# Later scatters and earlier routing in a fused RWKV attention and expert kernel

## The chip, the cores and the metric

One NeuronCore of a Trainium2 chip runs the whole kernel. The metric is device microseconds of one execution; the figure for a kernel is the median of its runs. Before the change that is 402.42 us (three runs, 400.07 to 404.3).

## The reference

Two stages. The first is RWKV attention over batch 4, 8 heads, 768 steps, head size 48; the second sends each of the 3072 resulting rows through the one of 8 experts with the highest gate logit (rows of 384, hidden width 1024, float32).

```python
def _attn_ref(r, k, v, w, u):
    ...
    for t in range(S):
        ...
        cur = np.einsum('bhd,bhe->bhde', u[None] * kt, vt)
        y[:, :, t] = np.einsum('bhd,bhde->bhe', rt, state + cur)
        state = wt[:, :, :, None] * state + np.einsum('bhd,bhe->bhde', kt, vt)

def _moe_ref(x, w_gate, w1, w2):
    logits = x @ w_gate
    expert_idx = np.argmax(logits, axis=1)
    ...
    for e in range(E):
        xe = x[expert_idx == e]
        out[expert_idx == e] = gate_w[..., None] * (np.maximum(xe @ w1[e], 0.0) @ w2[e])
```

## The kernel before

**Attention.** The 768 steps are cut into 12 chunks of 64. A block is one chunk of two of the four batches, so there are 24 blocks (`NB`) of 128 rows, and even and odd blocks carry separate states `U`. For a block n, VectorE (DVE) forms running products of the decays forwards (`pre`, L351) and backwards (`suf`, L360) and scales the keys, `kh` (L368). GpSimd (POOL) forms `rh` (r times `pre`, L395) and `rk` (r times k, L387). TensorE (PE) multiplies the old state by `rh` (`pe_inter`, L481), forms the block's score matrix from `kh` and `rh` (`pe_a`, tile `ap`, L466, 32 products), the bonus coefficients from `rk` (`pe_kt`, L512 and L522, whose copy by ScalarE (ACT) is `ct`, L413) and the transposed keys (L518). DVE copies the masked scores into the tile `at` (L373), which already holds the diagonals of coefficients that ACT (L432) and POOL (L423, `pool_diag`) wrote there. PE multiplies `at` by the values (`pe_av`, L491, tile `yp`) and adds the block to the state (`pe_dp`, tile `U`, L501). ACT copies `yp` out as the block's rows, `xr` (L452), and PE transposes them in the next iteration (L529, `xT`).

**Routing.** Four blocks make a group (`GRP`), six groups in all (`NG`). While the next group's blocks run, the finished group G is routed: gate logits on PE (`logit_mm`, L536, copied out as `ls`), their transposition (`logit_tr`, L543, tile `lt`), the maximum and the one-hot row on DVE (`gate`, L560 to L564), the rank within the expert on PE (`rank`, L575 to L578), the row number on DVE (`place`, L587 and L590, tile `pi`), and then four scatters (L604). A scatter is an indirect DMA that POOL issues: 128 rows of 386 floats of `xr` go to the places `pi` of the buffer `xs`, which is sorted by expert. A tiny memset on POOL (L609) follows each. Before any scatter, `xs` is filled with zero rows by eight stores on SyncE's (SP) queue, issued in iterations 0 to 5 (`prefill`, L335).

**Order.** PE, DVE, ACT and POOL execute in the order in which the program is written; SP too. `iteration(n)` writes, for n from -2 to 22, the work of block n on PE together with the preparation of blocks n+1 and n+2 on the other engines; i is n modulo 4. On POOL that is `rh` of n+1, a scatter if one is due, `rk` of n+2 and the diagonal of n+1. `rk` waits for `kh` of n+1 by a dependence marked "one port" in the code. Block 23 and the last routing follow by hand ("the hand-over"), among the first row tile of expert work: its load `xg` from `xs` (L260), its transposed copies (L300 to L302) and its first products (`mm1`, L311). Weights of an expert are split into a high and a low part on ACT and DVE in pieces (`side`, L237 and L239). From about 157 us on only expert work runs.

Of the kernel before, what the change touches and what calls it, by code (L numbers as in the profile page):

```python
# [12 lines left out]
AF = mybir.ActivationFunctionType  # L13
ALU = mybir.AluOpType
# [6 lines left out]
C = 64  # L21
NS = S // C
NB = NS * 2
# [9 lines left out]
GRP = 4  # L33
# [9 lines left out]
FIRST = 3  # L43
# [12 lines left out]
def rwkv_moe_kernel(ctx, tc, rkw, vv, ub, wg, wr, w1, w2, out):  # L56
    nc = tc.nc
# [306 lines left out]
    def dve_kh(n):  # L364
        if real(n):
            d = blk[n]
            d["kh"] = work([RP, NSEG, C], F32, "kh")
            ch["kh"] = nc.vector.tensor_tensor(out=d["kh"], in0=d["k"], in1=d["suf"][:, :, 3:SEG], op=ALU.mult)  # L368
# [19 lines left out]
            if n > 1:  # L388
                after(i, ch["kh"], "one port")

    def pool_rh(n):
        if real(n):
            d = blk[n]
            d["rh"] = work([RP, NSEG, C], F32, "rh")
            nc.gpsimd.tensor_tensor(out=d["rh"], in0=d["r"], in1=d["pre"][:, :, 1:C + 1], op=ALU.mult)  # L395

    def act_pad(n):
        if real(n) and (n // 2) % SUP:
# [11 lines left out]
    def act_ct(n):  # L410
        if real(n):
            blk[n]["ct"] = ct = sm.tile([P, H], F32, name="ct", tag="ct", bufs=3)
            nc.scalar.activation(ct, blk[n]["cp"], AF.Copy)  # L413

    def act_cT(n):
        if real(n):
# [37 lines left out]
    def act_xT(n):  # L454
        if real(n):
            blk[n]["xT"] = t = xtp.tile([P, DM], F32, name="xT", tag="xT")
            nc.scalar.activation(t, blk[n]["xp"], AF.Copy)

    def pe_a(n):
        if real(n):  # L460
# [63 lines left out]
    def pe_xT(n, t):  # L524
        if real(n):
            G, i = divmod(n, GRP)
            blk[n]["xp"] = xp = t[:, 0:DM]
            for j in range(3):
                nc.tensor.transpose(xp[:, j * P:(j + 1) * P], ch["xr", G][:, i, j * P:(j + 1) * P], ident)  # L529
# [68 lines left out]
    def pool_ids(G):  # L598
        nc.gpsimd.tensor_copy(ch["xr", G].bitcast(I32)[:, :, DM + 1], tokid[:, 2 * G:2 * G + 2, :].rearrange("p s b -> p (s b)"))

    def scatter(G, bs):
        xr = ch["xr", G]
        for b in bs:
            i = nc.gpsimd.indirect_dma_start(out=xsf, out_offset=bass.IndirectOffsetOnAxis(ap=ch["pi", G, b], axis=0),  # L604
                                             in_=xr[:, b, :], in_offset=None, bounds_check=E * NTOK - 1, oob_is_err=False)
            for k in scat:
                tc.declare_no_dep(i.ins, k, reason="rows of different tokens")
            scat.append(i.ins)
            nc.gpsimd.memset(none, 0.0)  # L609
# [80 lines left out]
    for n in range(1, LD):  # L690
# [3 lines left out]
        if n == 2:  # L694
            nc.sync.dma_start(wgt, wg)

    def iteration(n):
        G, i = divmod(n, GRP)
        g = G - 1 if n >= 0 else -1
        whole = (g, 0, GRP)  # L700
        if 0 <= n < 6:
            for e in range(E * n // 6, E * (n + 1) // 6):
                prefill(e)
        if n >= 0:
            load(n + 6)
        full = 0 <= g < NG - 1
        if real(n):
            blk[n]["ap"] = psA.tile([P, 4, 256], F32, name="ap", tag="ap")
            pe_xT(n - 1, blk[n]["ap"][:, 1:3, :].rearrange("p a c -> p (a c)"))
            pe_inter(n)  # L710
            pe_a(n)
        dve_scale(n + 1)
        if full and i == 2:
            gate(whole)
        if full and i == 3:
            place(whole)
        act_pend(n + 1)
        act_g(n + 1)
        pool_rh(n + 1)
        dve_suf(n + 1)  # L720
        if n == -2:
            pool_rk(0)
        pe_kt(n)
        act_pad(n + 2)
        dve_kh(n + 1)
        dve_at(n)
        act_kt(n)
        act_ct(n + 1)
        if full and i == 3:
            scatter(g, (0,))  # L730
        if g > 0 and i < 3:
            scatter(g - 1, ((1,), (2,), (3,))[i] if g - 1 != FIRST else ((1,), (2, 3), ())[i])
        if n > -2:
            pool_rk(n + 2)
        pe_av(n)
        if n < 2:
            act_diag(n + 1, range(0, H if n < 0 else NQ))
        act_xr(n)
        act_xT(n - 1)
        if n == NB - 2:  # L740
            dve_diag(n + 1)
        elif n >= 2:
            act_diag(n + 1, range(0, NQ))
        if n >= 0:
            pool_diag(n + 1)
        dve_pre(n + 2)
        pe_dp(n)
        if n >= 0:
            load_v(n + LV)
        if n == FIRST * GRP + 7:  # L750
            choose()
            eid[0] = expert_of(first[0:1, 0:1])
            feed()
        if full and i == 2:
            weigh(whole)
        if full and i == 0:
            logit_mm(whole)
        if full and i == 1:
            logit_tr(whole)
            pool_ids(g)  # L760
        if full and i == 2:
            rank(whole)
        if n == NB - 2:
            place(whole)
            scatter(g, (0, 1))
            side()
            side()
        if n == 3:
            late_constants()

# [64 lines left out]
    with tc.manual_schedule(engines={ET.PE, ET.DVE, ET.Activation, ET.Pool}):  # L835
# [13 lines left out]
        dve_at(z)  # L849
        halves(ua)  # L850
        transpose_rows(ua, 0)
        scatter(last - 1, (2, 3))
        pool_ids(last)
        pe_av(z)
        logit_mm(ka)
        act_xr(z)
        pe_xT(z, psA.tile([P, 4, 256], F32, name="xc", tag="ap")[:, 0:2, :].rearrange("p a c -> p (a c)"))
        act_xT(z)
        transpose_rows(ua, 1)
        logit_tr(ka)  # L860
        gate(ka)
# [328 lines left out]
```

## Time and profile before

| what | before |
|---|---|
| median of three runs | 402.42 us (400.07 to 404.3) |
| profiled execution | 402.55 us; span 400.9 us; 1.65 us around the span |
| PE busy | 367.1 us (92%) |
| DVE, ACT, POOL busy | 256.5, 195.9, 146.9 us |
| mean granted clock of TensorE | 0.955 |
| indirect scatters into `xs` | 24, 26.9 us of POOL |
| blocks of attention, hand-over, expert work | to 144, 144 to 157, 157 to 400 us |

A row of the timeline gives start, duration, engine, line, operation, output and inputs, the number of instructions in the row, and in brackets how long the engine sat idle before it and what ended that. "issue" means that nothing the profile shows was being waited for. PE is the matmul side of TensorE, PEld its weight loads, SPq the queue of SyncE. The clock is granted at one of two levels, 2.4 GHz (1.00 in the profile) and 1.2 GHz (0.50), and a stretch shows a mean of them.

### The profile page before, as it was taken

To read this page: it belongs to the slowest core of one execution; us is meant where nothing else is said; L and a number is where in the kernel's file an instruction comes from. 1 tells how busy PE (TensorE), PEld (TensorE's weight loads), DVE (VectorE), ACT (ScalarE), POOL (GpSimd) and SP (SyncE) were. 2 spreads that over 40 slices of the span, in tenths; PEclk is the share of its full clock that TensorE was granted. 3 is DMA by queue.
4 is the path that set the end of the run, shared out by engine and by line. 5 is a ranking of instruction groups with operands and counts; after the bars stand their busy time and mean duration, and the time that the engine had idled before them with its cause. 6 is when DMAs were issued, how large, how long until landed. Compare 5 with 4: busy or idle time off the path is not lost.

```text
span 400.9 us, 11609 instructions
## 1 busy us (share of the span) xinstructions
PE 367.1 (92%) x4642; PEld 333.4 (83%) x4642; DVE 256.5 (64%) x451; ACT 195.9 (49%) x516; POOL 146.9 (37%) x195
## 2 busy tenths in 40 slices
PE   7889798898989867999999999999999999999991
PEld 5667676676767656899899899999999999999991
DVE  7878877778768653668566456566476576683320
ACT  3656555565554633547365346455455564661300
POOL 4757477777766742211200040040050081105010
PEclk9999989999977895899999999999999999999997
DMA  8987788866622821579825456476466556721001
GB/s 216 247 247 215 206 229 237 231 201 201 179 87 73 273 81 54 177 240 315 244 76 187 126 148 200 131 203 210 125 190 226 176 130 219 252 81 32 26 17 42
DMA packets 38022, 67.64 MB, mean 169 GB/s; under 512 B 8141, under 2 KB 19714, under 8 KB 37962
## 3 DMA queue, kind: packets, MB, share of 16 engines
q1 hardware_dynamic: 31658, 57.33, 48.8%
q0 software_dynamic: 6304, 9.50, 7.5%
q8 instruction: 38, 0.62, 0.7%
q14 instruction: 22, 0.18, 0.2%
HBM read 55.34 MB, written 11.64 MB: 167 GB/s over the span
## 4 chain that ended last, share of the span: by engine, by line
PE 83%; ACT 5%; issue 5%; DVE 3%; another core or an unknown queue 1%; POOL 1%; POOLq 0%; ACTq 0%; DVEq 0%
PE N L325 14%; PE N L311 13%; PE cell L311 7%; PE mM L311 6%; PE N L970 6%; PE ap L466 4%; PE yp L491 4%; PE cell L970 3%; PE mM L970 3%; PE yp L481 3%; PE kp L518 3%; PE U L501 3%; PE ap L529 2%; PE N L300 2%; PE wrm L142 2%
## 5 line engine op out<-in xcount | busy, mean ns | idle before, releaser
L275 POOL DMA_INDIRECT out_dram<-ot,gi x16 | 22.2, 1390 | 103.2 <-issue 71.8
L275 POOL DMA_INDIRECT out_dram<-ort,gi x13 | 15.5, 1196 | 68.5 <-DVE ort L330 23.3
L325 PE MATMUL N<-w2h,hh 128*128 128x384 f32 (+4 forms) x104 | 35.9, 345 | 0.0
L387 POOL TENSOR_TENSOR rk<-rkwt 112x512 f32<-112x512 f32 x24 | 30.6, 1274 | 13.3 <-DVE kh L368 5.9
L325 PE MATMUL N<-w2l,hh 128*128 128x384 f32 (+4 forms) x104 | 35.0, 337 | 0.0
L325 PE MATMUL N<-w2h,hl 128*128 128x384 f32 (+4 forms) x104 | 35.0, 337 | 0.0
L239 DVE TENSOR_TENSOR w2l<-wst,w2h 128x512 fp32r<-128x512 f32 x48 | 32.1, 688 | 4.3 <-ACT w2h L237 3.9
L604 POOL DMA_INDIRECT xs<-xr,pi x24 | 26.9, 1119 | 21.6 <-issue 11.6
L314 DVE SCALAR_TENSOR_TENSOR hl<-N,hh 128x256 fp32r<-128x256 f32 (+8 forms) x37 | 19.4, 525 | 23.7 <-ACT hh L313 20.8
L239 DVE TENSOR_TENSOR w1l<-wst,w1h 128x512 fp32r<-128x512 f32 x48 | 33.1, 691 | 0.9 <-ACT w1h L237 0.4
L351 DVE TENSOR_TENSOR_SCAN pre<-rkwt,cell 112x536 f32<-112x536 f32 x24 | 30.4, 1268 | 1.1 <-DMA rkwt<-in_rkw_dram 0.6
L360 DVE TENSOR_TENSOR_SCAN suf<-rkwt,cell 112x536 f32<-112x536 f32 x24 | 30.4, 1265 | 0.4
L313 ACT ACTIVATE hh<-N 128x256 fp32r<-128x256 f32 (+8 forms) x37 | 17.3, 467 | 26.8 <-PE N L311 24.2
L237 ACT ACTIVATE w2h<-wst 128x512 fp32r<-128x512 f32 x48 | 28.4, 625 | 3.7 <-DMA wst<-in_w_dram 3.7
L237 ACT ACTIVATE w1h<-wst 128x512 fp32r<-128x512 f32 x48 | 29.7, 623 | 0.1
L395 POOL TENSOR_TENSOR rh<-rkwt,pre 112x512 f32<-112x512 f32 x24 | 29.3, 1219 | 0.0
L466 PE MATMUL ap<-rh,kh 48*64 48x64 f32 (+1 forms) x768 | 22.0, 227 | 7.9 <-issue 7.5
L311 PE MATMUL N<-xh,w1h 128*128 128x440 f32 (+6 forms) x84 | 28.8, 343 | 0.0
L311 PE MATMUL N<-xh,w1l 128*128 128x440 f32 (+6 forms) x84 | 28.6, 341 | 0.0
L311 PE MATMUL N<-xl,w1h 128*128 128x440 f32 (+6 forms) x84 | 28.6, 340 | 0.0
L373 DVE COPY_PREDICATED at<-cmask,ap 128x512 f32<-128x512 int32 x24 | 17.8, 742 | 16.6 <-PE ap L466 13.4
L418 ACT ACTIVATE cs<-yp 128x128 f32<-128x128 f32 x23 | 6.4, 277 | 39.9 <-PE yp L512 37.3
(200 smaller groups left out, 1002.0 us busy)
## 6 DMA issues: line engine op xcount, KB each, us to landing
wst<-in_w_dram SPq DMA_DIRECT2D x48, 256.0 KB
wst<-in_w_dram SPq DMA_DIRECT2D x16, 768.0 KB
rkwt<-in_rkw_dram SPq DMA_DIRECT2D x72, 96.0 KB
rkwt<-in_rkw_dram SPq DMA_DIRECT2D x24, 238.0 KB
vt<-in_vv_dram SPq DMA_DIRECT2D x48, 96.0 KB
wck_t<-in_wr_dram SPq DMA_DIRECT2D x6, 768.0 KB
rkwt<-in_rkw_dram SPq DMA_DIRECT2D x12, 224.0 KB
xg<-xs SPq DMA_DIRECT2D x4, 579.0 KB
```

Source lines behind the costliest of these rows:

```text
L237: nc.scalar.activation(hi, st[:, cs], AF.Copy)
L239: nc.vector.tensor_tensor(out=lo, in0=st[:, cs], in1=hi.bitcast(F32), op=ALU.subtract)
L275: i = nc.gpsimd.indirect_dma_start(out=out[:, :], out_offset=bass.IndirectOffsetOnAxis(ap=t.bitcast(I32)[0:rows.shape[0], q, 1:2], axis=0) ...
L311: nc.tensor.matmul(hp, a, x[p][:, j, :], start=(i == 0), stop=(i == 8))
L325: nc.tensor.matmul(op, a[:, cs], w2v(wt, w, f), start=(i == 0), stop=(i == 23))
L351: nc.vector.tensor_tensor_scan(out=d["pt"][:, 0, 0:NW], data0=d["w"], data1=cell[:RP, 0:1].broadcast_to([RP, NW]), initial=1.0, op0=ALU.mu ...
L360: nc.vector.tensor_tensor_scan(out=suf[:, ::-1], data0=d["w"][:, ::-1], data1=cell[:RP, 0:1].broadcast_to([RP, NW]), initial=1.0, op0=ALU. ...
L387: i = nc.gpsimd.tensor_tensor(out=d["rk"], in0=d["r"], in1=d["k"], op=ALU.mult)
L395: nc.gpsimd.tensor_tensor(out=d["rh"], in0=d["r"], in1=d["pre"][:, :, 1:C + 1], op=ALU.mult)
L466: nc.tensor.matmul(ap[half(b), 3 * j, q * C:(q + 1) * C], d["kh"][part(j), 2 * q + b, :], d["rh"][part(j), 2 * q + b, :], start=True, stop ...
L604: i = nc.gpsimd.indirect_dma_start(out=xsf, out_offset=bass.IndirectOffsetOnAxis(ap=ch["pi", G, b], axis=0), in_=xr[:, b, :], in_offset=No ...
L970: nc.tensor.matmul(pp, w, a, start=(i == 0), stop=(i == 23))
```

## The change

- Scatters in the loop: always one per iteration, written behind `rk` of n+2 and ahead of the diagonal of n+1, and waiting for the copy `ct` of block n+1 on ACT. A group's first scatter stands at i = 2 of the next group (before: i = 3), its fourth at i = 1. Before, they stood between `rh` and `rk` and waited for no engine of the block, and group 3's second and third shared one iteration.
- In an iteration after one with a scatter, `rh` of n+1 is written behind `kh` of n+1 and waits for it.
- Routing one block earlier: the transposed logits at i = 1 ahead of `pe_inter`, the gate on DVE at i = 1 between `kh` and the copy into `at`, the rank at the end of i = 1, the row numbers at i = 2.
- The choice of the first expert and the loads of its weights at n = 18 (before: 19).
- n = 22: one scatter of group 4, behind `rh` and ahead of the diagonal of block 23; the pieces of weight splitting stand around the copy into `at`. Before, two scatters and both pieces stood at the iteration's end.
- Hand-over: the three remaining scatters of group 4 stand behind ACT's copy `xT` of block 23 and wait for it, and the row identities (`pool_ids`) are written ahead of them. Before, two scatters stood ahead of the row identities.

```diff
@@ -388,11 +388,13 @@
             if n > 1:
                 after(i, ch["kh"], "one port")
 
-    def pool_rh(n):
+    def pool_rh(n, wait=False):
         if real(n):
             d = blk[n]
             d["rh"] = work([RP, NSEG, C], F32, "rh")
-            nc.gpsimd.tensor_tensor(out=d["rh"], in0=d["r"], in1=d["pre"][:, :, 1:C + 1], op=ALU.mult)
+            i = nc.gpsimd.tensor_tensor(out=d["rh"], in0=d["r"], in1=d["pre"][:, :, 1:C + 1], op=ALU.mult)
+            if wait:
+                after(i, ch["kh"], "one port")
 
     def act_pad(n):
         if real(n) and (n // 2) % SUP:
@@ -410,7 +412,7 @@
     def act_ct(n):
         if real(n):
             blk[n]["ct"] = ct = sm.tile([P, H], F32, name="ct", tag="ct", bufs=3)
-            nc.scalar.activation(ct, blk[n]["cp"], AF.Copy)
+            ch["ct"] = nc.scalar.activation(ct, blk[n]["cp"], AF.Copy)
 
     def act_cT(n):
         if real(n):
@@ -454,7 +456,7 @@
     def act_xT(n):
         if real(n):
             blk[n]["xT"] = t = xtp.tile([P, DM], F32, name="xT", tag="xT")
-            nc.scalar.activation(t, blk[n]["xp"], AF.Copy)
+            ch["xt"] = nc.scalar.activation(t, blk[n]["xp"], AF.Copy)
 
     def pe_a(n):
         if real(n):
@@ -598,11 +600,13 @@
     def pool_ids(G):
         nc.gpsimd.tensor_copy(ch["xr", G].bitcast(I32)[:, :, DM + 1], tokid[:, 2 * G:2 * G + 2, :].rearrange("p s b -> p (s b)"))
 
-    def scatter(G, bs):
+    def scatter(G, bs, behind=None):
         xr = ch["xr", G]
         for b in bs:
             i = nc.gpsimd.indirect_dma_start(out=xsf, out_offset=bass.IndirectOffsetOnAxis(ap=ch["pi", G, b], axis=0),
                                              in_=xr[:, b, :], in_offset=None, bounds_check=E * NTOK - 1, oob_is_err=False)
+            if behind is not None:
+                after(i, behind, "TensorE's dense products")
             for k in scat:
                 tc.declare_no_dep(i.ins, k, reason="rows of different tokens")
             scat.append(i.ins)
@@ -694,6 +698,11 @@
         if n == 2:
             nc.sync.dma_start(wgt, wg)
 
+    def moved(n):
+        G, i = divmod(n, GRP)
+        G -= 1 if i >= 2 else 2
+        return (G, ((i + 2) % GRP,)) if 0 <= G else ()
+
     def iteration(n):
         G, i = divmod(n, GRP)
         g = G - 1 if n >= 0 else -1
@@ -707,64 +716,65 @@
         if real(n):
             blk[n]["ap"] = psA.tile([P, 4, 256], F32, name="ap", tag="ap")
             pe_xT(n - 1, blk[n]["ap"][:, 1:3, :].rearrange("p a c -> p (a c)"))
+            if full and i == 1:
+                logit_tr(whole)
             pe_inter(n)
             pe_a(n)
         dve_scale(n + 1)
         if full and i == 2:
-            gate(whole)
-        if full and i == 3:
             place(whole)
         act_pend(n + 1)
         act_g(n + 1)
-        pool_rh(n + 1)
+        slow = moved(n - 1)
+        if not slow:
+            pool_rh(n + 1)
         dve_suf(n + 1)
         if n == -2:
             pool_rk(0)
         pe_kt(n)
         act_pad(n + 2)
         dve_kh(n + 1)
+        if slow:
+            pool_rh(n + 1, True)
+        if n == NB - 2:
+            scatter(*moved(n))
+        if full and i == 1:
+            gate(whole)
         dve_at(n)
+        if n == NB - 2:
+            side()
         act_kt(n)
         act_ct(n + 1)
-        if full and i == 3:
-            scatter(g, (0,))
-        if g > 0 and i < 3:
-            scatter(g - 1, ((1,), (2,), (3,))[i] if g - 1 != FIRST else ((1,), (2, 3), ())[i])
         if n > -2:
             pool_rk(n + 2)
         pe_av(n)
         if n < 2:
             act_diag(n + 1, range(0, H if n < 0 else NQ))
+        if n == NB - 2:
+            dve_diag(n + 1)
+            side()
         act_xr(n)
         act_xT(n - 1)
-        if n == NB - 2:
-            dve_diag(n + 1)
-        elif n >= 2:
+        if 2 <= n < NB - 2:
             act_diag(n + 1, range(0, NQ))
+        if moved(n) and n < NB - 2:
+            scatter(*moved(n), ch["ct"])
         if n >= 0:
             pool_diag(n + 1)
         dve_pre(n + 2)
         pe_dp(n)
         if n >= 0:
             load_v(n + LV)
-        if n == FIRST * GRP + 7:
+        if n == FIRST * GRP + 6:
             choose()
             eid[0] = expert_of(first[0:1, 0:1])
             feed()
-        if full and i == 2:
-            weigh(whole)
         if full and i == 0:
             logit_mm(whole)
         if full and i == 1:
-            logit_tr(whole)
+            weigh(whole)
             pool_ids(g)
-        if full and i == 2:
             rank(whole)
-        if n == NB - 2:
-            place(whole)
-            scatter(g, (0, 1))
-            side()
-            side()
         if n == 3:
             late_constants()
 
@@ -849,13 +859,13 @@
         dve_at(z)
         halves(ua)
         transpose_rows(ua, 0)
-        scatter(last - 1, (2, 3))
         pool_ids(last)
         pe_av(z)
         logit_mm(ka)
         act_xr(z)
         pe_xT(z, psA.tile([P, 4, 256], F32, name="xc", tag="ap")[:, 0:2, :].rearrange("p a c -> p (a c)"))
         act_xT(z)
+        scatter(last - 1, (1, 2, 3), ch["xt"])
         transpose_rows(ua, 1)
         logit_tr(ka)
         gate(ka)
```

The loop's first scatter on POOL, in iterations 6 and 7. Each `at` row is the diagonal that ends a block's POOL work, `xr_371` holds the rows of group 0, and `rk` is told by the buffer of loaded inputs that it reads, `rkwt`. Before, from the row identities of iteration 5 on:

```order
L599 COPY xr_371<-tokid_208 128x4
L395 TENSOR_TENSOR rh_1004<-rkwt_233,pre3_178 112x512
L387 TENSOR_TENSOR rk_1027<-rkwt_239 112x512
L423 TENSOR_TENSOR at_1048<-id2_189,ct_1025 128x256
L395 TENSOR_TENSOR rh_1124<-rkwt_239,pre3_178 112x512
L604 DMA xs_89<-xr_371,pi_1121 24576x386
L609 MEMSET none_215 1x1
L387 TENSOR_TENSOR rk_1151<-rkwt_246 112x512
L423 TENSOR_TENSOR at_1172<-id2_189,ct_1145 128x256
```

And with the change:

```order
L601 COPY xr_371<-tokid_208 128x4
L395 TENSOR_TENSOR rh_1018<-rkwt_233,pre3_178 112x512
L387 TENSOR_TENSOR rk_1041<-rkwt_239 112x512
L606 DMA xs_89<-xr_371,pi_1014 24576x386
L613 MEMSET none_215 1x1
L425 TENSOR_TENSOR at_1062<-id2_189,ct_1039 128x256
L395 TENSOR_TENSOR rh_1144<-rkwt_239,pre3_178 112x512
L387 TENSOR_TENSOR rk_1151<-rkwt_246 112x512
L606 DMA xs_89<-xr_371,pi_1014 24576x386
L613 MEMSET none_215 1x1
L425 TENSOR_TENSOR at_1172<-id2_189,ct_1149 128x256
```

The first scatter has moved from iteration 7 into iteration 6, ahead of the diagonal of block 7; in each iteration the scatter now stands behind `rk` in place of ahead of it. Later iterations of the loop read the same way.

The hand-over on POOL. `rh_2939` (with the change `rh_2965`) is that of block 23, the `at` row its diagonal, `xr_2244` holds group 4, `xr_2738` group 5 (its row identities), and `gi8` the row identities of the first row tile. Before:

```order
L395 TENSOR_TENSOR rh_2939<-rkwt_256,pre3_178 112x512
L423 TENSOR_TENSOR at_2975<-id2_189,ct_2954 128x256
L604 DMA xs_89<-xr_2244,pi_2990 24576x386
L609 MEMSET none_215 1x1
L604 DMA xs_89<-xr_2244,pi_2990 24576x386
L609 MEMSET none_215 1x1
L268 COPY gi8_224<-xg_2884 128x2
L604 DMA xs_89<-xr_2244,pi_2990 24576x386
L609 MEMSET none_215 1x1
L604 DMA xs_89<-xr_2244,pi_2990 24576x386
L609 MEMSET none_215 1x1
L599 COPY xr_2738<-tokid_208 128x4
```

And with the change:

```order
L395 TENSOR_TENSOR rh_2965<-rkwt_256,pre3_178 112x512
L606 DMA xs_89<-xr_2244,pi_2949 24576x386
L613 MEMSET none_215 1x1
L425 TENSOR_TENSOR at_2992<-id2_189,ct_2974 128x256
L268 COPY gi8_224<-xg_2902 128x2
L601 COPY xr_2738<-tokid_208 128x4
L606 DMA xs_89<-xr_2244,pi_2949 24576x386
L613 MEMSET none_215 1x1
L606 DMA xs_89<-xr_2244,pi_2949 24576x386
L613 MEMSET none_215 1x1
L606 DMA xs_89<-xr_2244,pi_2949 24576x386
L613 MEMSET none_215 1x1
```

One scatter of group 4 now stands ahead of the diagonal of block 23, and the other three behind both rows of identities.

## Rows read from the trace of the kernel before

**Rows 1.** The page: granted clock in tenths, in 40 slices of the span.

```profile
PEclk9999989999977895899999999999999999999997
```

**Rows 2.** The page: the chain that ended last, by engine.

```profile
PE 83%; ACT 5%; issue 5%; DVE 3%; another core or an unknown queue 1%; POOL 1%; POOLq 0%; ACTq 0%; DVEq 0%
```

**Rows 3.** Waits: engine, line, releaser; us in total, times, longest.

```profile
PE ap L466 <- issue: 7.5, 13, 1.5
```

**Rows 4.** Timeline: score products and what follows them, blocks 8 and 21.

```profile
55.85 0.66 PE L466 MATMUL ap<-rh,kh 64*64 64x64 f32 x32
...
56.45 0.42 PE L512 MATMUL yp<-rk,ubt 112*32 112x128 f32 x8
...
132.94 0.98 PE L466 MATMUL ap<-rh,kh 64*64 64x64 f32 x32
...
133.85 0.43 PE L512 MATMUL yp<-rk,ubt 112*32 112x128 f32 x8
```

**Rows 5.** Timeline: iteration 12, and the scatter of iteration 13.

```profile
78.03 1.01 POOL L604 DMA_INDIRECT xs<-xr,pi  x1 [0.16 <-DMA vt<-in_vv_dram]
...
79.40 0.51 PE L466 MATMUL ap<-rh,kh 48*64 48x64 f32 x17 [0.48 <-issue]
...
81.69 0.87 PE L501 MATMUL U<-vt,kt 128*48 128x96 f32 x16
...
81.78 0.61 POOL L423 TENSOR_TENSOR at<-id,ct 128x256 f32<-128x256 f32 x1 [1.39 <-ACT ct L413]
...
83.71 1.52 POOL L604 DMA_INDIRECT xs<-xr,pi  x1 [0.16 <-issue]
```

**Rows 6.** Timeline: score products of blocks 5 and 7, without a scatter near.

```profile
38.26 0.46 PE L466 MATMUL ap<-rh,kh 64*64 64x64 f32 x16 [0.55 <-issue]
...
49.89 0.69 PE L466 MATMUL ap<-rh,kh 48*64 48x64 f32 x30 [1.51 <-issue]
```

**Rows 7.** Timeline: the last zero stores, block 7's last products, the first scatter.

```profile
46.89 1.91 SPq L335 DMA_DIRECT2D xs<-zrow  x2
...
51.95 1.11 PE L491 MATMUL yp<-vt,at 64*64 64x48 f32 x32
...
52.51 1.21 POOL L604 DMA_INDIRECT xs<-xr,pi  x1 [4.81 <-DMA rkwt<-in_rkw_dram]
```

**Rows 8.** Timeline: iteration 21, behind its two scatters.

```profile
135.08 1.29 POOL L387 TENSOR_TENSOR rk<-rkwt 112x512 f32<-112x512 f32 x1
...
135.81 0.39 PE L522 MATMUL kp<-ident,cs 128*128 128x8 f32 x2 [1.01 <-ACT cs L418]
```

**Rows 9.** Timeline: block 22's end and the hand-over.

```profile
140.74 0.34 SPq L260 DMA_DIRECT2D xg<-xs  x1
...
143.14 0.85 POOL L423 TENSOR_TENSOR at<-id,ct 128x256 f32<-128x256 f32 x1 [4.33 <-ACT ct L413]
...
146.15 0.72 DVE L373 COPY_PREDICATED at<-cmask,ap 128x512 f32<-128x512 int32 x1
...
147.53 0.86 PE L536 MATMUL lp<-xT,wgt 128*32 128x128 f32 x18
...
150.08 0.97 POOL L604 DMA_INDIRECT xs<-xr,pi  x1 [0.22 <-issue]
...
151.80 0.27 ACT L539 ACTIVATE ls<-lp 96x128 f32<-96x128 f32 x1 [5.09 <-remote]
```

**Rows 10.** Windows: from, to, length, busy time of each engine, clock, DMA share, GB/s.

```profile
47.60:55.30 7.70, 5.82 (x130) 4.87 (x129) 5.08 (x9) 2.77 (x11) 2.88 (x5) 0.78 0.84 226
132.40:140.50 8.10, 6.98 (x139) 5.33 (x139) 4.22 (x8) 3.95 (x15) 5.64 (x8) 0.79 0.84 267
144.10:157.00 12.90, 7.93 (x142) 6.46 (x142) 5.14 (x17) 4.56 (x13) 5.08 (x10) 0.73 0.17 64
157.00:170.00 13.00, 12.27 (x78) 11.60 (x75) 7.54 (x29) 5.91 (x16) 4.21 (x8) 0.74 0.47 147
```

**Rows 11.** DMA issues: count, and median us from issue to landing.

```profile
xs<-xr,pi POOLq DMA_INDIRECT x24, 3.2
```

## The prediction

> **What bounds the kernel now.** I read the granted clock first, then the chain of waits, then the table of waits, and last the timeline of single iterations, because the change moves work within an iteration and only the timeline shows what stands beside what. The clock dips in three places only [rows 1]: around the first scatter, late in the attention, and at the hand-over to the experts. The chain is TensorE for 83%, ScalarE for 5%, and "issue" for another 5% [rows 2]. So a change on POOL can only pay where PE stood still without a wait of its own. One such place recurs: the score products `ap` paused for 7.5 us in 13 places with nothing to wait for [rows 3].
>
> Iteration 12 shows how the pause lies to a scatter. POOL issues the scatter from 78.03 to 79.04; the score products break off and go on at 79.40 after 0.48 us [rows 5]. Block 8 is the counterexample that helps: its scatter came after the score products, and the stretch from their first to the first product behind them is 56.45 - 55.85 = 0.60 us; block 21, with a scatter beside them, needs 133.85 - 132.94 = 0.91 [rows 4]. Summed over the 14 blocks 8 to 21, of which these two are the first and the last, that stretch is 10.7 us longer than 14 times 0.60. This sum is larger than the pauses, because the products on either side of a pause also run thinner. Against the scatter as the cause speak blocks 5 and 7 (and 6 between them, three in all, 2.7 us together): pauses of 0.55 and 1.51 us with no scatter at all [rows 6].
>
> **The change, part by part.** All sums start from the profiled execution, 400.9 us of span and 402.55 in all; it lies 0.13 above the median, so I take differences and do not correct for it.
>
> *Scatters behind `rk` and `ct`.* The instructions are the same in number; POOL issues one in 1.01 to 1.52 us [rows 5] wherever it stands. Their new place in iteration 12 would be from about 81.7, beside the states' update, which begins at 81.69 and lasts 0.87 [rows 5], and the transposes behind it. What the loop can get back is between 0 (the pauses are not the scatters') and -10.7 us (all of it). What is queued behind the waiting scatter is the diagonal of n+1, done so far at 81.78 + 0.61 = 82.39 [rows 5]; it moves to some 83.5, and the copy into `at` that needs it is written into the next iteration, whose own scatter began only at 83.71 [rows 5], so I cost it at nothing. If that cover goes, each microsecond of scatter lengthens its block. I take -5, the middle: the blocks with a scatter have most of the pauses, but the three blocks without one show that part of them will stay.
>
> *`rh` behind the keys.* It adds no work. `rh` and `rk` now run back to back behind `kh`; `rk` takes 1.29 us [rows 8], and `rh`, of the same shape, is put at the same, 2.6 together, which ends before `ct` in an undisturbed iteration. `rh` of n+1 is needed only in the next block. Zero, if the iteration does not shrink below POOL's own sum.
>
> *The pair of scatters in iteration 21.* Two scatters ahead of `rk` made it start at 135.08 and the coefficients' second product wait 1.01 us [rows 8], and the clock granted in that stretch was 0.79 with 6.98 us of PE busy [rows 10]. With one scatter, and behind `rk`, the wait goes: -1.0, and at full clock 6.98 x 0.21 = up to -1.5. I take -2, bounds 0 and -2.5.
>
> *The first scatter, one iteration earlier.* It writes `xs`, which the zero stores fill. The last two stores are issued at 46.89 and take 1.91 on the queue; the first scatter, though first in line on POOL, starts only at 52.51 after 4.81 us of waiting [rows 7]. The row names a load of inputs as the releaser, but the buffer it writes is that of the stores, and I take them to set its start. Moving the scatter one iteration up does not move the stores. POOL now sits on it in iteration 6 with the diagonal of block 7 queued behind: scatter to 52.51 + 1.21 = 53.72, diagonal 0.61 [rows 5] behind a memset of about 0.1, copy into `at` 0.72 [rows 9], so the products with the values start near 55.2 in place of 51.95 [rows 7]: +3.2. The clock in this stretch is 0.78 already [rows 10]; a longer idle PE may cost more of it. Bounds +2 (part regained in blocks 8 and 9, whose `rk` no longer queue behind scatters) and +7; I take +3.5.
>
> *Routing one block earlier, and the first weights.* The same instructions on PE and ACT; on DVE the gate's three short operations stand before the copy into `at` instead of before `suf`. Zero, hidden behind PE; price if not, a few tenths in six groups. The first weights' loads go ahead of one load of values; DMA share is well below full late in the attention, and I cost that at nothing too.
>
> *Hand-over.* Before, logits were done at 147.53 + 0.86 = 148.39, but ACT copied them out at 151.80, after 5.09 us idle by a releaser that the profile cannot name; POOL's fourth scatter began at 150.08 and ended at 151.05 [rows 9]. This is the only place on the chain where a train of scatters ends shortly before a release. With the three scatters behind the last `xT`, the copy should follow the logits: -3.4. If the hold comes with any train of scatters it moves along to the next step on ACT: 0. On the other side one scatter now stands ahead of block 23's diagonal and waits until the first row tile has been read from `xs`, a load issued at 140.74 [rows 9]. If that lands after as long as the scatters, 3.2 us [rows 11], the scatter runs from 143.94 to 145.4 and the diagonal (0.85) ends at 146.3, against a copy into `at` that began at 146.15 [rows 9]: a few tenths. I take -2.3 in all, bounds +1.4 and -5; the last would need part of the lower clock of 144 to 170 us (0.73 and 0.74 [rows 10]) to come back as well.
>
> Sum: -5 - 2 + 3.5 - 2.3 = -5.8, so 402.55 - 5.8 = 396.7 us.
>
> **The rivals.**
>
> *The pauses are not the scatters'.* For it: rows 6. Then the loop gives 0 and the rest is -2 + 3.5 - 2.3 = -0.8: 401.8 us. The Trainium skill ("SBUF — State Buffer", section "SBUF: two separate sides") states such a rule: engine ports and DMA ports are disjoint, so that a DMA cannot be slowed by a compute operation, nor the other way round. By that rule moving a scatter away from the score products gives nothing, and the time is 401.8; here the row of iteration 12 speaks against it and rows 6 for it. Chance 0.20.
>
> *The first scatter costs more than its wait.* PE idle for longer there, half clock for the next block: +7 instead of +3.5, the rest as forecast, 400.2. Chance 0.10.
>
> *Slower: the scatter reaches the next block.* `rh`, `rk`, scatter, memset and diagonal are 1.29 + 1.29 + 1.01 to 1.52 + about 0.1 for the memset + 0.61 = 4.3 to 4.8 us of POOL behind each `kh`. Where `kh` comes late, the scatter slips onto the next block's products and holds the diagonal. It decides once the scatter starts over 2 us behind `ct`. Then each of 16 scatters costs the pause of 0.48 us [rows 5] again on top of the old ones, 7.7 us: 402.55 - 0.8 + 7.7 = 409.4. Against it: in iteration 12 POOL waited 1.39 us for `ct` before the diagonal [rows 5]. Chance 0.12; half of it reaches only 404 to 406.
>
> *Everything comes back.* -10.7 - 2.5 + 3.2 - 3.4 = -13.4: 389.2. Chance 0.12.
>
> **How the numbers follow.** The forecast has 0.46, and its own range is 393 to 399.5. A measurement of this kernel can tell about 1%, 4 us, from no change. Faster by more than that means under 398.4: nine tenths of the forecast's 0.46 and the 0.12 of full recovery, with a little of the two middle rivals, 0.55. Slower means over 406.4: 0.10, with a little from the middle rivals, 0.13. The rest, 0.32, lies within. The range that leaves out 2 in 10 reaches from full recovery into the lower half of the slower rival: 389.5 to 404.
>
> **What would show it.** Score products next to their followers by 0.6 us in blocks 8 to 21, with the scatter rows beginning behind `ct`, confirm the loop's term; pauses of the same size elsewhere on PE (update, transposes, state products) refute it. The first scatter waiting some 6 us in iteration 6, and block 7's products with the values near 55 us, confirm the +3.5. The logits' copy close behind the logits confirms the hand-over; a new wait of 3 us on the next ACT step refutes it. The coefficients' second product of block 21 must lose its wait. I am wrong on the whole if the attention ends later than 144 us, or if the diagonals become what DVE's copy waits for.

## The result and the profile after

The change made the kernel a little slower: ratio to before 1.0057 (95% interval 1.0032 to 1.0082), medians 402.48 and 400.07 us over 22 runs each. Every ratio here compares only executions in the faster of the two states that a kernel shows. The forecast was 396.7, 1.5% faster. The profiled execution of the change took 404.09 us with a span of 402.3, against 402.55 and 400.9: 1.4 us of span to account for.

The page of the change: chain by engine, and granted clock.

```profile
PEclk9999969999999995799999999999999999999998
...
PE 79%; ACT 5%; DMA 4%; DVE 4%; issue 3%; SPq 2%; POOL 1%; POOLq 0%; ACTq 0%; DVEq 0%
```

Against [rows 1, 2], the dips late in the attention are gone, the first one (slice 6) is deeper, the one at the hand-over (slices 16 and 17) is still there, and "issue" fell from 5% to 3%. In its place "DMA" stands with 4%: on that chain 7.5 us ahead of block 23's diagonal (iteration 21's scatter, landing after 4.48 us, and behind it the first row tile's load, 3.04 us), 1.9 us ahead of the first scatter, and the rest at the kernel's start. Cut at the starts of the same blocks, the windows say where the time went. Columns are as in [rows 10]; first the kernel before, then the change.

```profile
47.59:55.35 7.76, 5.88 (x130) 4.88 (x129) 5.12 (x9) 2.83 (x11) 2.94 (x5) 0.78 0.83 225
66.58:132.44 65.86, 59.10 (x1516) 47.29 (x1515) 51.65 (x81) 37.00 (x134) 47.40 (x59) 0.92 0.58 170
144.10:156.93 12.83, 7.86 (x142) 6.39 (x142) 5.07 (x16) 4.56 (x13) 5.08 (x10) 0.73 0.17 64
156.93:170.29 13.36, 12.63 (x80) 11.96 (x79) 7.90 (x29) 6.20 (x16) 4.23 (x9) 0.75 0.46 143
```

```profile
48.20:60.38 12.18, 5.72 (x130) 4.62 (x130) 4.38 (x7) 3.50 (x12) 5.92 (x8) 0.73 0.80 225
71.88:133.82 61.94, 54.30 (x1509) 43.09 (x1509) 52.93 (x81) 36.92 (x132) 48.02 (x60) 1.00 0.67 196
143.19:154.95 11.76, 8.16 (x142) 6.35 (x142) 3.87 (x13) 3.48 (x10) 4.24 (x10) 0.77 0.17 61
154.95:171.79 16.84, 14.92 (x81) 13.96 (x79) 8.17 (x29) 5.98 (x16) 5.37 (x11) 0.66 0.40 140
```

Row by row: block 7 (4.42 us longer), blocks 10 to 20 (3.92 shorter), block 23 to the first expert product (1.07 shorter), first products to second layer (3.48 longer). Between them, block 7 starts 0.61 later, blocks 8 and 9 take 0.27 more, block 21 takes 2.56 less (5.49 for 8.05) and block 22 0.27 more. The sum is +1.5; from the second layer on both kernels take 230.6 and 230.5 us. Part of the gain in blocks 10 to 20 is clock: they ran at 0.92 before and at 1.00 in the change (third column from the end).

**The first scatter**, in the change's timeline:

```profile
48.10 1.04 SPq L335 DMA_DIRECT2D xs<-zrow  x2
...
54.26 1.20 POOL L606 DMA_INDIRECT xs<-xr,pi  x1 [8.69 <-DMA rkwt<-in_rkw_dram]
...
55.53 0.61 POOL L425 TENSOR_TENSOR at<-id,ct 128x256 f32<-128x256 f32 x1
...
56.18 0.73 DVE L373 COPY_PREDICATED at<-cmask,ap 128x512 f32<-128x512 int32 x1 [5.98 <-POOL at L425]
...
56.96 1.04 PEld L493 LDWEIGHTS yp<-vt,at 64*64 64x64 f32 x32 [6.55 <-DVE at L373]
56.96 1.21 PE L493 MATMUL yp<-vt,at 64*64 64x48 f32 x32 [6.46 <-DVE at L373]
```

Read upwards: PE waits 6.46 us for the copy into `at`, that for the diagonal, that for the scatter, and the scatter for the stores, which SP issued at 48.10 (before 46.89 [rows 7]). Nothing on DVE or PE is late by itself.

**A scatter in its new place**, iteration 21:

```profile
134.32 0.66 PE L468 MATMUL ap<-rh,kh 64*64 64x64 f32 x32
134.91 0.43 PE L514 MATMUL yp<-rk,ubt 112*32 112x128 f32 x8
...
135.74 0.39 PE L524 MATMUL kp<-ident,cs 128*128 128x8 f32 x2
...
137.05 1.01 POOL L606 DMA_INDIRECT xs<-xr,pi  x1 [1.56 <-ACT ct L415]
```

The score products follow through in 0.59 us (0.91 in [rows 4]), the coefficients' second product has lost its wait of [rows 8], and the scatter starts behind `ct`. Over the kernel the pauses of [rows 3] went from 7.5 us in 13 places to this:

```profile
PE ap L468 <- issue: 3.7, 7, 1.8
```

This total mixes two kinds of pause. Number PE's matmuls and weight loads from the start of the kernel. In the fourteen profiles of this study, PE makes 103 pauses of over 0.15 us with nothing to wait for, all of them in the attention. 74 of them stand at the same place in every 256 numbers, give or take one, on score products and others alike, with a scatter near or not. The pauses of blocks 5 to 7 [rows 6], at numbers 1473, 1729 and 1986, are of this kind. The other 29 all begin during a scatter or within 0.4 us of its end, and only they follow the scatters' place:

| profiles | at the recurring numbers | at a scatter |
|---|---|---|
| before | 7 pauses, 5.8 us | 9 pauses, 3.0 us |
| e4 (old place) | 4, 2.8 us | 8, 3.3 us |
| the change | 5, 4.1 us | 4, 0.7 us |
| e1, e2, e3 (new place) | 3 to 6, 1.4 to 4.2 us | 1 to 4, 0.2 to 0.7 us |
| e5 to e9, r1 to r3 (new place) | 4 to 9, 2.1 to 6.2 us | none |

What holds PE at the recurring numbers no run tests. The page of either kernel lists 38 transfers on a queue that it calls "instruction", and PE has some 9280 matmuls and weight loads, so a wait for its own instructions is the first thing to look at.

**The hand-over**, where [rows 9] stood before:

```profile
141.74 0.34 SPq L260 DMA_DIRECT2D xg<-xs  x1
...
145.58 1.04 POOL L606 DMA_INDIRECT xs<-xr,pi  x1 [3.30 <-DMA xg<-xs]
...
146.67 0.62 POOL L425 TENSOR_TENSOR at<-id,ct 128x256 f32<-128x256 f32 x1
...
147.33 0.72 DVE L373 COPY_PREDICATED at<-cmask,ap 128x512 f32<-128x512 int32 x1 [3.56 <-POOL at L425]
...
148.11 0.78 PE L493 MATMUL yp<-vt,at 64*64 64x48 f32 x32 [2.85 <-DVE gi L270]
...
148.82 0.96 PE L538 MATMUL lp<-xT,wgt 128*32 128x128 f32 x18
...
149.82 0.27 ACT L541 ACTIVATE ls<-lp 96x128 f32<-96x128 f32 x1 [4.13 <-PE lp L538]
...
159.61 0.41 PE L311 MATMUL N<-x,w1l 128*128 128x256 f32 x1
...
162.37 0.38 ACT L313 ACTIVATE hh<-N 128x256 fp32r<-128x256 f32 x1 [4.20 <-PE N L311]
...
166.21 0.39 PE L311 MATMUL N<-x,w1l 128*128 128x256 f32 x1 [1.54 <-DVE w1l L239]
```

The copy of the logits now follows them at once. But two new waits stand there. Block 23's last products wait 2.85 us; their row names DVE's next small operation, but what they need is the copy into `at` that ended just before it, and the diagonal of that copy stood behind the scatter. And ACT's copy `hh` of the second piece starts at 162.37, though its last product began at 159.61 and took 0.41. The split weights queue behind that copy, PE waits 1.54 us for a low part, and the mean clock from the first product to the second layer is 0.66. It was at its upper level until PE had stood still for block 23's copy:

```profile
146.00:148.00 2.00, 0.00 (x0) 0.00 (x0) 0.67 (x2) 0.00 (x0) 1.54 (x5) 1.00 0.26 99
148.00:150.00 2.00, 1.67 (x50) 1.24 (x50) 0.61 (x4) 0.18 (x2) 0.00 (x0) 0.86 0.00 0
150.00:152.00 2.00, 1.48 (x7) 1.48 (x8) 0.00 (x0) 1.01 (x4) 0.00 (x0) 0.50 0.00 0
```

### The profile page after: what moved, and what is told of

Its sections match the earlier page's. It is cut to its first block, busy times and chain, and to the rows that moved or that the text cites. A ratio compares the mean times of both kernels' runs of the same rounds, so it can differ in the third digit from the quotient of the medians.

```text
span 402.3 us, 11594 instructions
## 1 busy us (share of the span) xinstructions
PE 362.9 (90%) x4641; PEld 329.7 (82%) x4642; DVE 257.4 (64%) x451; ACT 195.7 (49%) x516; POOL 145.9 (36%) x195
## 4 chain that ended last, share of the span: by engine, by line
PE 79%; ACT 5%; DMA 4%; DVE 4%; issue 3%; SPq 2%; POOL 1%; POOLq 0%; ACTq 0%; DVEq 0%
PE N L311 14%; PE N L325 14%; PE cell L311 7%; PE mM L311 6%; PE N L980 6%; PE yp L493 4%; PE cell L980 3%; PE mM L980 3%; PE ap L468 3%; PE yp L483 3%; DMA rkwt<-in_rkw_dram 3%; PE ap L531 3%; PE kp L520 2%; PE U L503 2%; PE N L300 2%
## 5 line engine op out<-in xcount | busy, mean ns | idle before, releaser
L606 POOL DMA_INDIRECT xs<-xr,pi x24 | 24.4, 1016 | 24.0 <-DMA rkwt<-in_rkw_dram 8.7
L493 PE MATMUL yp<-vt,at 64*64 64x48 f32 x768 | 18.2, 226 | 12.7 <-DVE at L373 9.6
L493 PEld LDWEIGHTS yp<-vt,at 64*64 64x64 f32 x768 | 15.2, 137 | 14.1 <-DVE at L373 10.6
```

Source lines behind the costliest of these rows:

```text
L493: nc.tensor.matmul(d["yp"][half(b), j, q * D:(q + 1) * D], d["at"][half(h), j, q, :], d["v"][half(h), h, (j * NQ + q) * D:(j * NQ + q + 1) ...
```

## The experiments

Ratios are to the kernel before in the same rounds. e1 to e4 ran together, e5 to e8 together on another chip, r1 to r3 and e9 together. Their kernel before took 399.4, 393.2 and 394.5 us, so ratios are compared, and differences of a few tenths of a per cent only within a set. Each kernel has one profile, so a time read from a profile is that of one execution.

**e1: zero stores earlier.**

```diff
-        if 0 <= n < 6:
-            for e in range(E * n // 6, E * (n + 1) // 6):
+        if 0 <= n < 4:
+            for e in range(2 * n, 2 * n + 2):
```

> The change, with the eight zero stores issued two per iteration in iterations 0 to 3 (before: iterations 0 to 5). Theory A (the loss is the first scatter, which holds the diagonal of block 7 until the stores have landed; the changed trace shows it start at 54.26 and block 8 at 60.38 against 55.35 before): the first scatter starts near 47, block 8 near 53, and the time falls by 4 to 6 us against the change, to about 0.99 of before. Theory B (the loss is at the hand-over, from PE's signals arriving late): ratio to before stays at 1.003 to 1.008. Theory C (stores compete with the blocks' loads): blocks 2 to 5 start later by as much as block 8 gains, ratio 1.00 to 1.006.

0.9943 (0.9904 to 0.9981), 1.1% below the change. The scatter's wait is now 1.31 us, and it ends with a copy on ACT and not with a DMA:

```profile
47.16 1.21 POOL L606 DMA_INDIRECT xs<-xr,pi  x1 [1.31 <-ACT xT L459]
...
50.36 0.78 PE L493 MATMUL yp<-vt,at 64*64 64x48 f32 x32
```

Block 7 takes 4.93 us in place of 12.18, and blocks 2 to 6 start within 0.8 us of the change's. This is theory A. It also speaks for the stores as the releaser of [rows 7], and not the load that the row names: moving the stores removed the wait.

**e2: block 22 and hand-over as before.**

```diff
-        if n == NB - 2:
-            scatter(*moved(n))
...
+        if n == NB - 2:
+            scatter(NG - 2, (0, 1))
+            side()
+            side()
...
+        scatter(last - 1, (2, 3))
         pool_ids(last)
...
-        scatter(last - 1, (1, 2, 3), ch["xt"])
```

> The change, with block 22 and the hand-over as before (two scatters of group 4 at the end of iteration 22, two behind the expert tile's first transposes). Theory A (the hand-over is worth little in either direction, the first scatter is the loss): ratio to before 1.002 to 1.009. Theory B (the hand-over of the change loses 2 to 4 us, since block 23's diagonal waits for the scatter behind the first row tile's load, and seven scatters run beside the first products): ratio 0.994 to 0.999.

1.0008 (0.9971 to 1.0045), between the two theories, so it does not price the hand-over. The first products to the second layer take 13.37 us again (16.84 in the change), and the logits' copy waits 5.2 us again.

**e3: the scatters' place in the loop, and `rh` behind the keys, on the kernel before.**

```diff
+        slow = due(n - 1)
+        if not slow:
+            pool_rh(n + 1)
...
+        if slow:
+            pool_rh(n + 1, True)
...
-            scatter(g, (0,))
...
+        if due(n):
+            scatter(*due(n), ch["ct"])
```

Here `due(n)` gives the scatters that the kernel before had in iteration n.

> The kernel before, with only the scatters' place in the loop changed: behind rk of n+2, waiting for ct of n+1, and rh behind kh in the iteration after one with a scatter; which scatter runs in which iteration, the routing and the hand-over stay as before. Theory A (score products paused for the scatters, moving them gains 5 to 7 us in blocks 9 to 21, and the first scatter in iteration 7 holds only the diagonal of block 8): ratio 0.983 to 0.992. Rival (the pauses are not the scatters'): 0.997 to 1.003.

0.9911 (0.9868 to 0.9955): the place together with `rh`'s wait gains 0.9%. Of the 2.1 us of pauses that are left, 2.0 stand at the recurring numbers. The second row is blocks 10 to 20.

```profile
PE ap L468 <- issue: 2.1, 4, 0.9
...
61.45:122.05 60.60, 54.54 (x1515) 43.76 (x1514) 51.32 (x82) 36.71 (x131) 46.20 (x60) 1.00 0.69 202
```

**e4: the change with the scatters in the old place, and `rh` never behind the keys.**

```diff
-        slow = moved(n - 1)
+        slow = ()
...
+        if moved(n) and n < NB - 2:
+            scatter(*moved(n))
         if n > -2:
             pool_rk(n + 2)
```

> The change, with the loop's scatters back between rh and rk, no wait for ct, rh never behind kh; one scatter per iteration and one block earlier as in the change. Theory A: the first scatter still holds POOL from iteration 6, and the pauses of the score products return: 1.012 to 1.022 of before. Rival (the place of the scatters is worth nothing): as the change, 1.003 to 1.008.

1.0111 (1.0048 to 1.0173), just under the range of theory A. Part of it is not the pauses: the first scatter now also holds `rk`, and block 7 takes 14.08 us. The pauses came back in number, 8 of the 11 at a scatter, and blocks 10 to 20 took 64.51 us where the change took 61.94, both at full clock:

```profile
PE ap L468 <- issue: 5.2, 11, 1.3
...
72.54:137.05 64.51, 55.89 (x1510) 43.87 (x1509) 51.69 (x81) 36.85 (x132) 48.17 (x59) 1.00 0.64 185
```

**e5: e1, with all four scatters of group 4 behind the last `xT`.**

```diff
-        if n == NB - 2:
-            scatter(*moved(n))
...
-        scatter(last - 1, (1, 2, 3), ch["xt"])
+        scatter(last - 1, (0, 1, 2, 3), ch["xt"])
```

> e1 (the change with early zero stores) with group 4's scatter of iteration 22 moved behind the last xT too, so that block 23's diagonal waits for no scatter and four scatters stand there in place of three. Theory A (the scatter that waited 2.6 us for the first row tile's load held the diagonal, the copy and block 23's last products by 2.2 us): PE's wait for that copy goes, block 23 to the first expert products takes about 9 in place of 10.9 us. Theory B (the late signal of PE during the train decides): the train is one scatter longer, first products to second layer stays at 17 us or grows; ratio within 0.003 of e1. By A alone the ratio falls by 0.005.

0.9876 (0.9837 to 0.9915). Block 23 to the first expert product takes 7.15 us, less than theory A's 9, and the clock stays up through both stages. The third row, from the second layer to the end, shows that 4.6 us are given back there (e1: 230.5 us). In time e5 cannot be told from e6, of the same set.

```profile
134.61:141.76 7.15, 6.15 (x141) 4.81 (x142) 3.39 (x12) 3.04 (x10) 1.26 (x3) 1.00 0.10 37
141.76:153.52 11.76, 10.06 (x80) 9.22 (x79) 9.00 (x32) 6.54 (x17) 7.97 (x16) 1.00 0.63 203
153.52:388.70 235.18, 222.90 (x1308) 217.11 (x1306) 132.04 (x244) 105.08 (x213) 39.91 (x38) 0.99 0.50 155
```

**e6: e1 with e2's edit.**

> e1 with block 22 and the hand-over as before. Theory (from the traces of before, the change and the first four runs): the first products to the second layer take 13.4 in place of 17.0 us, the logits' copy waits 3 to 5 us again, block 23 to first products 12.8 in place of 10.9; net 1 to 2 us less than e1: ratio 0.988 to 0.993. Rival (the loss at the first products is chance of one execution): no change against e1, 0.994.

0.9894 (0.9852 to 0.9936), as forecast, but not by the forecast way: on this chip the logits' copy did not wait, and first product to second layer took 13.26 us. The clock was 0.80 from block 23 to the first product and 0.87 behind it, though PE had no wait of 0.8 us or more between block 23's start and the first product.

**e7: e1, with group 4's three scatters behind group 5's.**

```diff
-        scatter(last - 1, (1, 2, 3), ch["xt"])
...
         scatter(last, (3,))
+        scatter(last - 1, (1, 2, 3))
         mm1(ua, 1)
```

> e1 with the three scatters of group 4 behind those of group 5 instead of ahead of them, so that POOL starts its train only when group 5's row numbers are there, some 4 us later, and no scatter stands beside the first two pieces of the first products. Theory (a train of scatters makes PE's signals late, and the copy hh that waits for the signal starts 2.3 to 2.7 us late, then the weight pieces behind it): hh of the second piece follows its products at once, the late signal moves behind it into a stretch with more slack, first products to second layer 14 to 15.5 us. Rival (the late signal does not depend on the train): still about 2.5 us at the second piece, 17 us.

0.9984 (0.9943 to 1.0024). Inconclusive for its question: neither copy was late in any profile of this set. Its profile lost time elsewhere: blocks 21 and 22 took 12.82 us (e6: 9.35), and the part from the second layer on 235.8 (e6: 232.3). The second row tile's load, which stands behind the later train, is 0.59 us of that; the rest is not explained.

**e8: e3 without moving `rh`.**

```diff
-        slow = due(n - 1)
+        slow = ()
```

> e3 (only the scatters' place in the loop changed) without moving rh behind kh: rh stands at the iteration's start always. Theory A (the gain is the scatters' place and rh's wait is neutral): as e3, 0.987 to 0.996. Rival (rh beside the backward scan or kh slows DVE, so the wait is part of the gain): DVE's kh longer than 0.69 us where rh runs, blocks longer by 0.3 to 0.5 us, ratio 0.995 to 1.003.

0.9988 (0.9951 to 1.0025), the rival's number: the place without `rh`'s wait shows no gain in the whole time. Against e3 it is of another chip, on which the kernel before has no profile, so only the trace can say how much of the difference is `rh`. The rows are `kh` beside `rh` ahead of block 21's products, `kh` of the next block alone, a pause, and blocks 10 to 20:

```profile
125.76 1.18 POOL L395 TENSOR_TENSOR rh<-rkwt,pre 112x512 f32<-112x512 f32 x1
...
126.03 1.47 DVE L368 TENSOR_TENSOR kh<-rkwt,suf 112x512 f32<-112x512 f32 x1
...
132.41 0.24 PE L503 MATMUL U<-vt,kt 128*48 128x96 f32 x1 [2.30 <-issue]
...
134.68 0.69 DVE L368 TENSOR_TENSOR kh<-rkwt,suf 112x512 f32<-112x512 f32 x1
...
64.55:126.31 61.76, 54.75 (x1515) 43.81 (x1514) 53.41 (x81) 36.95 (x134) 46.51 (x60) 0.97 0.66 188
```

`kh` beside `rh` takes 1.47 us; over blocks 8 to 21 `kh` takes 14.0 us here and 10.3 in e3. Blocks 10 to 20 are 1.2 us longer than in e3, which would make the wait of `rh` worth about 0.1 us a block; and they are 4.1 us shorter than before and 2.8 shorter than in e4, with no pause at a scatter, which speaks for a gain of the place without it. The rest of the difference between e3 and e8 is not explained by `rh`: e8 had two long blocks (7 and 21: 7.42 and 8.58 us), and each holds a pause at the recurring numbers (1.51 and 2.30 us).

**r1, r2, r3: the change, e1's and e6's kernels on one chip.**

> The change itself, on the chip and in the rounds of the three that follow, so that each of its parts is priced against it directly. Theory (first scatter +5, hand-over +2, loop -6): 1.003 to 1.009 of before; first scatter waits 7 to 9 us, block 7 to 8 takes 11 to 13 us. Rival for the hand-over (the late signal of PE is of the chip that ran, and not of the order): the copy of the second piece starts within 0.5 us of its products on a chip where the hand-over of before shows no late signal either.

> The change with early zero stores, beside the change on one chip. Theory (the first scatter's wait for the stores): 4 to 6 us, 0.010 to 0.015 of ratio, below the change. Rival: under 0.004.

> The same with the hand-over of before, beside the two above. Theory (the change's hand-over loses): 0.003 to 0.006 below the kernel with early zero stores alone. Rival (no loss by the order): within 0.003 of it.

1.0038 (0.9993 to 1.0083), 0.9917 (0.9874 to 0.9960), 0.9848 (0.9782 to 0.9914). So early stores are worth 0.012 (4.8 us), and the old hand-over some 0.007 more (2.7 us). The intervals of the last two ratios overlap; compared directly, the mean of r3's executions lies 2.4 us below that of r2's (95% interval 0.7 to 4.2). r3 has the lowest ratio of the study, but e5's and e9's intervals overlap with its own. The windows from block 23 to the first product, to the second layer and to the end, first r2, then r3:

```profile
133.34:144.40 11.06, 7.99 (x141) 6.52 (x142) 3.87 (x13) 3.48 (x10) 4.23 (x10) 0.78 0.14 50
144.40:158.45 14.05, 13.58 (x80) 12.91 (x79) 8.08 (x29) 6.20 (x16) 5.50 (x11) 0.68 0.50 164
158.45:389.00 230.55, 220.62 (x1308) 215.43 (x1306) 132.54 (x244) 105.61 (x213) 40.20 (x37) 0.99 0.50 156
```

```profile
132.86:140.74 7.88, 6.28 (x141) 4.98 (x142) 3.51 (x11) 4.07 (x12) 4.90 (x10) 1.00 0.29 104
140.74:152.48 11.74, 10.03 (x80) 9.22 (x79) 8.97 (x32) 6.54 (x17) 4.20 (x8) 1.00 0.47 136
152.48:386.40 233.92, 221.78 (x1308) 215.38 (x1306) 132.16 (x244) 104.89 (x213) 39.93 (x38) 0.99 0.50 155
```

In r2 neither copy is late, and yet the hand-over costs 5.5 us more than in r3 (25.11 against 19.62): the wait for block 23's diagonal is there, as in this row of r2, and the clock falls to 0.78 and 0.68.

```profile
136.87 0.72 DVE L373 COPY_PREDICATED at<-cmask,ap 128x512 f32<-128x512 int32 x1 [2.95 <-POOL at L425]
```

r3 gives 3.4 us back later, 233.92 against 230.55 us, so about 2 us of the 5.5 reach the end.

**e9: e3 with all four scatters of group 4 behind the last `xT`.**

```diff
-            scatter(g, (0, 1))
...
-        scatter(last - 1, (2, 3))
         pool_ids(last)
...
+        scatter(last - 1, (0, 1, 2, 3), ch["xt"])
```

> Routing as before, only the scatters' place in the loop changed (as e3), and all four scatters of group 4 behind the last xT, so that none stands ahead of the logits or of block 23's diagonal. Theory (routing one block earlier gains nothing, and the hand-over loses by the scatter that holds the diagonal): 0.985 to 0.991 of before, the fastest of the four. Rival (routing earlier is part of the gain): 0.993 to 0.998.

0.9900 (0.9835 to 0.9964), as the theory had it but for the order: not faster than r3. Blocks 9 to 12 and 13 to 16 take 20.73 and 20.96 us, those of r3 20.60 and 21.40, so routing one block earlier shows neither gain nor cost there; r2, with the same loop as r3, took 22.79 and 21.33, so a difference of a microsecond would not be seen. e9 shows the next bound:

```profile
155.62 0.37 PE L300 MATMUL N<-ident,xg 104*128 104x104 f32 x2 [0.69 <-DMA xg<-xs]
```

PE comes to the second row tile before its load, which must wait for the last scatter.

## Why the prediction was wrong

- **Scatters in the loop: right.** Forecast -5. Measured -3.92 in blocks 10 to 20, and +0.27 in blocks 8 and 9. The stretch from the first score product to the first product behind them, over blocks 8 to 21, went from 10.2 us above 14 times 0.60 (the prediction's 10.7 is a slip in the sum) to 3.7, and those blocks together from 85.1 to 78.9 us. e4 has the pauses back, and its stretch is 10.0 us above. That -5 came out so near is chance in part: it was the middle of 0 to -10.7, and a part of the -3.92 is the clock, which the step did not count. The rival that the pauses are not the scatters' holds for one kind of pause: the 4.8 us in 5 places of [rows 3] that stand at the recurring numbers, rows 6 among them. It fails for the other kind, 2.7 us in 8 places. The rule of the Trainium skill quoted for that rival ("SBUF — State Buffer", section "SBUF: two separate sides") would have the move gain nothing; the pauses at a scatter, 9 before and 1 in e3, speak against using it so. By which path a scatter makes PE pause, no run shows.
- **Iteration 21: right.** Forecast -2, measured -2.56 (block 21's 5.49 against 8.05), just past the bound of -2.5.
- **First scatter: right in kind, too small.** Forecast +3.5; +4.42 in block 7 and +0.61 ahead of it. The sum took the stores' landing from before; SP issued them 1.2 us later, and the scatter started at 54.26, not 52.51. e1 and r2 price it at 4.6 and 4.8 us.
- **`rh` behind the keys: costed at zero, and worth something.** e8 shows what it prevents: `kh` of 1.47 us in place of 0.69 where `rh` runs beside it.
- **Hand-over: this step failed.** Forecast "-2.3 in all"; measured -1.07 + 3.48 = +2.4. The logits' copy did come 3.4 us sooner after its products, as forecast. But the step put the scatter ahead of block 23's diagonal at "a few tenths", from a start at 143.94 and a diagonal done at 146.3, against a copy at 146.15. The first row tile's load was issued at 141.74, a microsecond later than the 140.74 that the step took from before: on the chain it stands behind the landing of iteration 21's scatter, which the change itself had moved back. It released the scatter of iteration 22 after 3.84 us in place of 3.2. So the scatter started at 145.58 and the copy at 147.33. The comparison was at fault too: before, the copy at 146.15 stood behind two pieces of weight splitting on DVE, which the change moved away. These two rows of the kernel before say so, and that PE idled 0.86 us for it, where it now idles 2.85:

```profile
144.93 1.29 DVE L239 TENSOR_TENSOR w1l<-wst,w1h 128x512 fp32r<-128x512 f32 x2
...
146.92 0.68 PE L491 MATMUL yp<-vt,at 64*64 64x48 f32 x32 [0.86 <-DVE at L373]
```

  And the step counted the lower clock only as something that might come back. Here it fell to its lower level behind PE's wait, and the first expert products ran at 0.66. Two of the prediction's own signs came true: the next ACT step (`hh`) had the new wait, and a diagonal became what DVE's copy waits for, in block 7 (5.98 us) and in block 23 (3.56 us).
- **What stays open:** why ACT's copy `hh` came 2.3 us late in the change, 2.4 in e1 and 3.9 in e4, and the logits' copy late in before, e2 and e3. In these six profiles the order of scatters at the hand-over decided which copy it was. In the profiles of the later sets neither copy was late, with the same orders, so the scatters alone do not make it. r2 against r3 shows that a loss stands without it: 5.5 us at the hand-over, of which about 2 reach the end. How much of the 4.7 us missed at the hand-over is the late copy, the wait or the clock, no run separates; e6 and r3, one kernel on two chips, differ there by 2.1 us with a clock of 0.80 and 0.87 against 1.00.

The sum missed by about 7 us: 4.7 at the hand-over, 1.5 at the first scatter, the rest in the loop and in blocks 21 and 22.

## What to carry to other kernels

Before an asynchronous issue is moved ahead of other work on its queue, ask what its operands wait for at the new place, and who is queued behind: here one scatter waited 8.69 us for stores and another 3.30 us for a load, and both had a diagonal behind them that bounded the block. Compare a moved step with when its consumer could run, not with when it ran before. Where a bubble (idle time) goes in front of long dense work, add what it may cost in clock. And before pauses are put down to one cause, count the instructions between them: here one total held two kinds.

## What the runs showed of the hardware

- Beside the issue of a POOL scatter a row of small products on PE paused 0.2 to 0.6 us with nothing to wait for: 9 times, 3.0 us in all, before, and 8 times, 3.3 us, in e4; once, 0.2 us, with the scatters behind the products (e3).
- Apart from that PE paused, for 0.15 to 2.3 us, at one place in every 256 of its matmuls and weight loads: 74 pauses in fourteen profiles, whatever the scatters did.
- A DVE product of two SBUF inputs took 1.47 us beside a POOL product, and 0.69 alone. The Trainium skill ("SBUF — State Buffer", section "SBUF: two separate sides") has the shared port of GpSimd and VectorE taken by one instruction at a time; the row agrees: `kh` began 0.27 us into `rh`, which lasted 1.18, and ended 0.56 us behind it, a little less than the 0.69 it takes alone.
- From the first expert product to the second layer the granted clock was 0.66, 0.72 and 0.68 (the change, e1, r2) where PE had waited 2.2 to 2.9 us for block 23's copy, and 1.00 in e5, e8, e9 and r3, where no wait in block 23 reached 1 us. That wait is not all of it: e4, e6 and e7, without it, had 0.80, 0.87 and 0.87.
